# A cheaper exponential on VectorE for 94 tiles, a fused mixer step and zero-weight filler matmuls in a two-layer transformer kernel

## The chip, the cores and the metric

The kernel runs on one core of a Trainium2 chip. The core has a matrix engine (TensorE, PE in the profile; its weight loads are listed as PEld), a vector engine (VectorE, DVE), a scalar engine for activation functions (ScalarE, ACT), a general engine (GpSimd, POOL) and a queue engine (SyncE, SP) that issues the transfers. They run side by side, each working through its own list of instructions in order, and wait for one another by semaphores. The metric is the device time of one execution in microseconds (us).

## The reference

The sequence has 2048 rows of 448 numbers. Two layers with the same weights are applied; each has an attention block A and a mixer block B, and each block gets a layer norm of the stream and is added to it:

```python
def _A_ref(x, wqkv, wo):          # 16 heads of 28
    q, k, v = split(x @ wqkv)
    p = _softmax(einsum("bhqd,bhkd->bhqk", q, k) * 28 ** -0.5)
    return merge(einsum("bhqk,bhkd->bhqd", p, v)) @ wo

def _B_ref(x, w1, w2, w3, w4):
    h = _gelu(_layernorm(x) @ w1)
    hs = concatenate([h quarters shifted by -1, +1, -2, +2 rows]) @ w2
    x1 = x + hs
    h2 = _gelu(_layernorm(x1) @ w3) @ w4     # 448 -> 1792 -> 448
    return x1 + h2

x = A_x
for layer in range(2):
    x = x + _A_ref(_layernorm(x), A_wqkv, A_wo)
    x = x + _B_ref(_layernorm(x), B_w1, B_w2, B_w3, B_w4)
```

The mixer block is thus given a normalised x, and its own sum x1 starts from that. The GELU is the tanh approximation. Inputs and outputs are bf16.

## The kernel before

**Tiling.** The 2048 rows are 16 row tiles of 128. The stream lies in `x_res` (bf16, 128 x 16 x 448) in on-chip memory for the whole run. Heads are handled in 4 groups of 4; the 4 heads of a group use the four 32-row strips of PE at once. Scores are computed transposed (keys on partitions, 512 query columns), so one score tile is 128 keys x 512 queries of one head, and there are 2048 such tiles in the two layers.

**The attention pipeline.** `t_attention` (L1703 ff.) walks over 821 groups of score tiles. Groups have in turn three and two tiles, which fill banks 0 to 2 and 3 and 4 of the accumulator memory. For group n PE computes the scores (L1722), ACT takes the exponential of the whole group in one instruction into `PT` (L1748), and PE multiplies the result with the values (`t_pv`, L1781; the sums of four heads stay in bank 5, `UBK`). The scores of group n+2 are computed into the banks of group n as soon as these have been read, while ACT works on group n+1.

**The exponential on VectorE.** For the groups in `DVE_TILES` (76 of them) ACT does the first two tiles only and VectorE the third, in `t_dexp` (L1631 ff.). The score is a power of two with an offset. Five instructions make the bits of a bf16 number: L1633 turns the score into a fixed-point integer (`t32`, one buffer) and so frees the bank; L1643 takes the low 16 bits, the fraction f, times a constant; L1644 and L1645 make a cubic correction from it, with two half buffers `gt0` and `gt1` of `gt`, which `tanh_gelu` of the mixer uses too; L1648 adds integer and correction and writes 16 bits into `PTD`. The product with the values is deferred by four groups for such a tile. A score matmul into the third bank waits for L1633 of the group two back.

**The mixer.** `t_mixA` takes the row means and variances (L1278, L1279) and normalises (L1958) for w1; `t_r1` makes the reciprocal root R1 of a row. `t_x1` makes x1 for one row tile: L2027 writes (x - mean) x R1 into `x1b` (fp32); PE multiplies the shifted GELU output with w2; L2046 adds it from the accumulator; L2049 to L2053 make the statistics of x1; L2055 adds `x1b` to `x_res`; L2057 normalises for w3. `t_mixB` multiplies with w3, evicts (L2094, DVE; L2091, ACT in the last tiles), ACT takes the GELU of several row tiles at once (`t_gelu`, L2134), PE multiplies with w4, and the result is added to `x_res` (L2117) or, in the last layer, to the output buffer (L2110), which SP stores.

**What sets the order.** All steps are generators that yield instructions. A planner runs twice; then `follow` reorders each engine's list by numbers written out in `ENGINE_ORDER` and moves some choices (`OTHER`) between ACT and DVE. While it lays out PE's list it calls `keep_pe_busy` (L340 ff.), which puts filler matmuls into stretches that the planner's durations show as empty: 128 x 256 of ones into an accumulator bank that is free (L2169), while the planned use of the last 4 us is under 80%. Where no bank is free there is no filler. These durations only set the order; at run time every engine waits for semaphores alone.

Of the kernel before, what the change touches and what calls it, by code (L numbers as in the profile page):

```python
# [49 lines left out]
class Place(str):  # L50


    KINDS = {"b": 8, "sq": 2, "x1b": 2, "xn": 2, "xT": 2, "gw": 2, "gt": 2, "ob": 2, "ti": 1, "pd": 3}
# [163 lines left out]
class Sched:  # L217
# [122 lines left out]
    def keep_pe_busy(self, until):  # L340
# [3 lines left out]
        if self.pe_mode not in (None, "plain"):  # L344
            idle = max(self.strip_free) + self.SW
            if max(self.cur["pe"], idle) + dur + 0.12 >= until:
                return
            self.cur["pe"] = max(self.cur["pe"], idle)
        while self.cur["pe"] + dur + 0.12 < until:
            t = self.cur["pe"]  # L350
# [5 lines left out]
            pick = None  # L356
            for b in banks:
                if key(b) in self.live:
                    continue
                ds = self.P.deps("pe", reads, [key(b)])  # L360
                if all(d.t_end + self.LAT <= t + 0.02 for d in ds.values()):
                    pick = b
                    break
            if pick is None:
                self.cur["pe"] = t + 0.1
                continue
            self.P.add("pe", lambda e, b=pick: fn(e, b), reads, [key(pick)], t_end=t + dur)
            self.recent.append((t, t + dur))
            self.log.append(("pe", t, t + dur, "fill"))
            self.cur["pe"] = t + dur  # L370
            self.pe_mode = "plain"
            self.strip_free = [self.cur["pe"]] * 4
# [203 lines left out]
    def follow(self, order, other, banks):  # L576
# [27 lines left out]
        new.landed = 0.0  # L604
        P = new.P
        made = {}
        head = {e: 0 for e in ENGS}
        while len(made) < len(ops):
# [51 lines left out]
            else:  # L660
                if e == "pe":
# [3 lines left out]
                    new.strip_free, new.begun = pe[3], pe[4]  # L665
                elif e == "act" and kw.get("tab") is not None:
                    new.act_tab = kw["tab"]
# [45 lines left out]
def build_kernel(nc, A_x, A_wqkv, A_wo, B_x, B_w1, B_w2, B_w3, B_w4, out, n_layers=2):  # L713
    S = A_x.shape[1]
    D = 448
# [16 lines left out]
    EXPA = (0.07826797 * 128) ** (1 / 3)  # L732
    EXPB = EXPA * 0.30457565 / 0.07826797
# [1527 lines left out]
```

## Time and profile before

| | |
|---|---|
| time, median of 3 runs | 1041.9 us (1039.48 to 1047.28) |
| the profiled execution: time, span | 1048.76 us, 1047.0 us |
| ACT busy | 1005.5 us, 96% |
| PE busy (matmul) | 974.1 us, 93% |
| DVE busy | 812.6 us, 78% |
| POOL busy | 57.7 us, 6% |
| mean granted PE clock | 0.980 |

Busy time is the time in which an engine executes something; PE's is modelled, since matmuls overlap in its pipeline. The span runs from the first to the last instruction. A row of the groups names the line of the kernel, the engine, the operation, what it writes and reads, how often it ran, the busy time, the mean duration in ns, and the engine's idle time just before with who ended it. A row of the waits names who waited, for whom, how long in total, how often and how long at most. The granted clock is the share of the full clock at which PE ran.

### The profile page before, as it was taken

Reading aid. Unit: us, or ns where it says so; the run is one execution under the profiler, and the core shown is the slowest. Engines: PE = TensorE matmul, PEld = TensorE weight load, DVE = VectorE, ACT = ScalarE, POOL = GpSimd, SP = SyncE. Lnnn points to the kernel's source line nnn. Section 1 sums busy time; section 2 is a strip of 40 time slices with the busy share of each in tenths; the row PEclk is TensorE's granted clock in tenths of the full one; section 3 lists DMA queues with packets and bytes.
Section 4 is the critical chain, followed back from the end, with each engine's and each line's share of the span. In section 5 each row is a group of like instructions: output and inputs, shape, how many; then the busy total and the mean of one; then the engine's idle time right before and its main releaser. Section 6 shows DMA issues by size and latency. Waiting matters only on the chain.

```text
span 1047.0 us, 23598 instructions
## 1 busy us (share of the span) xinstructions
PE 974.1 (93%) x10240; PEld 369.3 (35%) x10260; DVE 812.6 (78%) x1809; ACT 1005.5 (96%) x942; POOL 57.7 (6%) x80
## 2 busy tenths in 40 slices
PE   8998898989998999999999999988898999999998
PEld 4332222323232243332343443323333233443456
DVE  8977667877888778889788777788988846876674
ACT  7999879999999999999999999999999999999984
POOL 2000000000001001010000000000011000010000
PEclk9999769999999999999999999999999999999999
DMA  5246002001011002101111101311010100110000
GB/s 138 62 124 161 11 12 49 2 16 21 1 39 21 1 2 41 36 2 22 22 52 31 27 11 49 105 41 41 21 37 1 21 19 10 26 22 2 14 3 27
DMA packets 70720, 35.19 MB, mean 34 GB/s; under 512 B 56472, under 2 KB 65048, under 8 KB 70616
## 3 DMA queue, kind: packets, MB, share of 16 engines
q1 hardware_dynamic: 70616, 33.68, 13.5%
q8 instruction: 80, 1.31, 0.5%
q14 instruction: 24, 0.20, 0.1%
HBM read 12.70 MB, written 7.08 MB: 19 GB/s over the span
## 4 chain that ended last, share of the span: by engine, by line
ACT 79%; PE 19%; DVE 1%; DMA 1%; issue 0%; SPq 0%; DVEq 0%
ACT PT L1748 72%; PE ps L1128 6%; PE ps L1722 4%; ACT h2T L2134 4%; PE ps L1781 3%; PE ps L1131 3%; PE ps L1391 1%; ACT gt L1918 1%; PE ps L2169 1%; ACT L2134 1%; DMA wk_raw<-in_A_wqkv_dram 1%; ACT L1748 0%; PE ps L1336 0%; DVE hT L1885 0%; ACT vaug L1461 0%
## 5 line engine op out<-in xcount | busy, mean ns | idle before, releaser
L1748 ACT ACTIVATE PT<-ps 128x1024 bf16<-128x1024 f32 (+1 forms) x821 | 903.0, 1235 | 14.8 <-PE ps L1722 11.3
L1781 PE MATMUL ps<-PT,vaug 128*32 128x512 bf16 (+1 forms) x2221 | 287.8, 369 | 4.1 <-ACT PT L1748 2.6
L1722 PE MATMUL ps<-qT,kT 32*128 32x512 bf16 x1536 | 248.8, 393 | 39.7 <-ACT PT L1748 33.3
L1722 PEld LDWEIGHTS ps<-qT,kT 32*128 32x128 bf16 x1536 | 60.4, 91 | 246.6 <-ACT PT L1748 178.1
L1781 PEld LDWEIGHTS ps<-PT,vaug 128*32 128x32 bf16 x2221 | 82.8, 95 | 121.9 <-issue 78.6
L2094 DVE CAST h2T<-ps 128x512 bf16<-128x512 f32 (+2 forms) x126 | 72.3, 582 | 38.3 <-PE ps L1131 19.7
L1128 PE MATMUL ps<-xT,w 112*128 112x512 bf16 (+6 forms) x483 | 99.2, 318 | 1.4 <-DVE h2T L2094 0.7
L1722 PE MATMUL ps<-kT 32*128 32x256 bf16 (+1 forms) x768 | 83.4, 310 | 13.5 <-ACT PT L1748 11.4
L1131 PE MATMUL ps<-xT,w 112*32 112x512 bf16 (+3 forms) x1172 | 90.8, 346 | 0.5 <-DVE h2T L2094 0.4
L2169 PE MATMUL ps<-ones_bf 128*128 128x256 bf16 x402 | 75.0, 293 | 4.9 <-DVE ones_bf L1158 2.7
L1633 DVE TENSOR_SCALAR t<-ps 128x512 int32<-128x512 f32 x76 | 52.2, 687 | 28.4 <-PE ps L1722 27.6
L1131 PE MATMUL ps<-w,h2T 128*32 128x448 bf16 x948 | 60.3, 353 | 2.0 <-ACT h2T L2134 1.6
L1648 DVE SCALAR_TENSOR_TENSOR PTD<-t,gt 128x512 uint16<-128x512 int32 x76 | 52.2, 687 | 3.0 <-PE ps L1781 1.3
L1128 PEld LDWEIGHTS ps<-xT,w 112*128 112x128 bf16 (+1 forms) x483 | 39.3, 104 | 41.3 <-issue 21.6
L1645 DVE SCALAR_TENSOR_TENSOR gt<-gt 128x512 f16<-128x512 f16 x76 | 52.0, 685 | 1.5
L1644 DVE SCALAR_TENSOR_TENSOR gt<-gt 128x512 f16<-128x512 f16 x76 | 51.9, 683 | 1.3
L1128 PE MATMUL ps<-w,h2T 128*128 128x448 bf16 x211 | 52.1, 355 | 0.0
L1722 PEld LDWEIGHTS ps<-kT 32*128 32x128 bf16 x768 | 23.1, 91 | 78.5 <-ACT PT L1748 60.5
L1391 PE MATMUL ps<-xT,wq_raw 112*32 112x512 bf16 (+1 forms) x576 | 49.2, 366 | 0.6 <-DVE gt L1643 0.3
L2169 PEld LDWEIGHTS ps<-ones_bf 128*128 128x128 bf16 x402 | 33.6, 102 | 43.8 <-issue 19.7
L2134 ACT ACTIVATE h2T<-h2T 128x7168 bf16<-128x7168 bf16 (+2 forms) x9 | 44.9, 5012 | 0.1
L1391 PE MATMUL ps<-xT,wk_raw 112*32 112x512 bf16 (+3 forms) x640 | 43.8, 339 | 0.2 <-DVE hT L1885 0.2
(145 smaller groups left out, 1092.8 us busy)
## 6 DMA issues: line engine op xcount, KB each, us to landing
uin<-uscr SPq DMA_DIRECT2D x20, 256.0 KB, 2.6
uscr<-u_sb SPq DMA_DIRECT2D x12, 256.0 KB, 2.0
uscr<-uin SPq DMA_DIRECT2D x8, 256.0 KB, 2.3
out_dram<-uin SPq DMA_DIRECT2D x16, 112.0 KB, 1.7
w<-in_B_w_dram SPq DMA_DIRECT2D x4, 392.0 KB, 5.4
x_res<-in_A_x_dram SPq DMA_DIRECT2D x3, 448.0 KB, 8.3
w<-in_B_w_dram SPq DMA_DIRECT2D x2, 448.0 KB, 4.7
w<-in_B_w_dram SPq DMA_DIRECT2D x4, 196.0 KB, 6.6
```

The source lines that it names most:

```text
L1128: return e.matmul(out=dst(0, m), lhsT=lhs(0, m), rhs=rhs() if callable(rhs) else rhs, start=start, stop=stop)
L1131: return [e.matmul(out=dst(a, min(m, a + 32)), lhsT=lhs(a, min(m, a + 32)), rhs=rhs() if callable(rhs) else rhs, start=start, stop=stop, t ...
L1391: yield op("pe", c_mm(nw) + Sched.COLT, lambda e, b=b, fc=fc, rows=rows: [e.matmul(out=ps[32 * j:32 * j + 32, bi(b), 0:nw], lhsT=w[0:rows, ...
L1633: yield op("dve", 0.06 + c_ps(512), lambda e: e.tensor_scalar(out=t32[:, :], in0=ps[:, bk, :], scalar1=0.0, scalar2=65536.0, op0=ALU.max, ...
L1645: yield op("dve", c_ps(512), lambda e: e.scalar_tensor_tensor(out=half(x), in0=half(f), scalar=EXPB, in1=half(x), op0=ALU.add, op1=ALU.mul ...
L1648: yield op("dve", 0.06 + c_ps(512), lambda e: e.scalar_tensor_tensor(out=PTD[:, to.n, :].bitcast(mybir.dt.uint16), in0=t32[:, :], scalar=2 ...
L1722: yield op("pe", 0.005 if ph == h else 0.012 + W / 2400.0, lambda e, bk=bk, r0=32 * j, g=g, kc=kc, qt=qt, q0=q0, W=W, c0=W * h: e.matmul(o ...
L1748: yield op("act", e_dur(n), lambda e, b0=b0, p0=p0, cnt=cnt: e.activation(out=PT[:, p0:p0 + cnt, :], in_=ps[:, b0:b0 + cnt, :], func=ACT.E ...
L1781: return e.matmul(out=ps[32 * j:32 * j + 32, UBK, 0:128 * nt], lhsT=vaug[:, vs, 32 * (4 * g + j):32 * (4 * g + j) + 32], rhs=rhs(), start= ...
L2094: yield op("dve", c_ps(NW), lambda e, fch=fch, b=b: e.tensor_copy(out=h2T[:, fch, hoff:hoff + NW], in_=ps[:, bi(b), 0:NW]), reads=[("ps", ...
L2134: yield op("act", c_act(14 * NW), lambda e, c0=c0, NW=NW: e.activation(out=h2T[:, :, c0:c0 + NW], in_=h2T[:, :, c0:c0 + NW], func=ACT.Gelu ...
L2169: SC.fill = (0.13, lambda e, b: e.matmul(out=ps[:, bi(b), 0:256], lhsT=ones_bf[:, :], rhs=ones_bf[:, :].unsqueeze(1).to_broadcast([128, 2, ...
```

## The change

It has five parts.

1. **The exponential on VectorE** has another form of the cubic: a linear step, its square (a product of the buffer with itself), and a step that adds a constant and multiplies with the fraction. It needs one half buffer instead of two, so two tiles can be under way; `t32` gets a second buffer as well. The number of instructions stays five.
2. **94 tiles** instead of 76 go to VectorE.
3. **The mixer's first branch.** x x R1 + hs is made in one step straight from the accumulator, without subtracting the mean. x1 then carries a constant per row (mean x R1), which the later layer norms remove by themselves. The stream keeps this constant; `t_r1` collects it in `OFF`, and the last step subtracts it. `x1b` becomes bf16.
4. **Zero-weight filler.** Where no accumulator bank is free, `keep_pe_busy` adds, to the sums in bank 5 that are open (begun and not ended), a matmul of 32 columns of zero weights per strip.
5. **The order** of all engines is written anew.

```diff
-    KINDS = {..., "gt": 2, "ob": 2, "ti": 1, "pd": 3}
+    KINDS = {..., "gt": 2, "ob": 2, "ti": 2, "pd": 3}
...
             for b in banks:
                 if key(b) in self.live:
                     continue
                 ds = self.P.deps("pe", reads, [key(b)])
                 if all(d.t_end + self.LAT <= t + 0.02 for d in ds.values()):
-                    pick = b
+                    self.P.add("pe", lambda e, b=b: fn(e, b), reads, [key(b)], t_end=t + dur)
+                    self.pe_mode = "plain"
                     break
-            if pick is None:
-                self.cur["pe"] = t + 0.1
-                continue
+            else:
+                opened = [j for j in range(4) if 0 < self.sums[j] < self.summands]
+                if not opened or t + self.SW + dur + 0.12 >= until:
+                    t += 0.1
+                    continue
+                for j in opened:
+                    self.P.add("pe", lambda e, j=j: self.still(e, j), self.still_reads, [(self.sum_key, (j, "still"))], t_end=t + dur)
+                self.pe_mode = "col4"
...
-            ti = yield ("acq", ["ti0"])
+            ti = yield ("acq", ["ti0", "ti1"])
...
-            f = yield ("acq", ["gt0"])
-            x = yield ("acq", ["gt1"])
-            ... tensor_scalar(out=half(f), in0=lo, scalar1=EXPA * 2.0 ** -16, scalar2=None, op0=ALU.mult)
-            ... scalar_tensor_tensor(out=half(x), in0=half(f), scalar=-EXPA, in1=half(f), op0=ALU.add, op1=ALU.mult)
-            ... scalar_tensor_tensor(out=half(x), in0=half(f), scalar=EXPB, in1=half(x), op0=ALU.add, op1=ALU.mult)
+            x = yield ("acq", ["gt0", "gt1"])
+            ... tensor_scalar(out=half(), in0=frac(), scalar1=EXPS * 2.0 ** -24, scalar2=EXPH * 2.0 ** -8, op0=ALU.mult, op1=ALU.add)
+            ... tensor_tensor(out=half(), in0=half(), in1=half(), op=ALU.mult)
+            ... scalar_tensor_tensor(out=half(), in0=half(), scalar=EXPV * 2.0 ** -16, in1=frac(), op0=ALU.add, op1=ALU.mult)
...
-        x1b = sb("x1b", [128, NX1, D], FP32)
+        x1b = sb("x1b", [128, NX1, D], BF16)
...
+            yield op("dve", 0.1, ... tensor_tensor(out=mst[:, sl, MR if L else OFF], in0=mv[:, sl, 0], in1=mst[:, sl, R1], op=ALU.mult)
+            if L:
+                yield op("dve", 0.1, ... tensor_tensor(out=mst[:, sl, OFF], in0=mst[:, sl, OFF], in1=mst[:, sl, MR], op=ALU.add)
...
-            yield op("dve", ... tensor_scalar(out=x1b[:, s.n, :], in0=x_res[:, t, :], scalar1=mv[:, t, 0:1], scalar2=mst[:, t, R1:R1 + 1], op0=ALU.subtract, op1=ALU.mult)
...
-            yield op("dve", ... tensor_tensor(out=x1b[:, s.n, :], in0=x1b[:, s.n, :], in1=ps[:, bi(hb), 0:D], op=ALU.add)
+            yield op("dve", ... scalar_tensor_tensor(out=x1b[:, s.n, :], in0=x_res[:, t, :], scalar=mst[:, t, R1:R1 + 1], in1=ps[:, bi(hb), 0:D], op0=ALU.mult, op1=ALU.add)
...
-                    yield op("dve", ... tensor_tensor(out=obf(o), in0=x_res[:, t, :], in1=ps[:, bi(b), 0:D], op=ALU.add)
+                    yield op("dve", ... scalar_tensor_tensor(out=obf(o), in0=x_res[:, t, :], scalar=mst[:, t, OFF:OFF + 1], in1=ps[:, bi(b), 0:D], op0=ALU.subtract, op1=ALU.add)
...
+            SC.still = lambda e, j: e.matmul(out=ps[32 * j:32 * j + 32, UBK, 0:256], lhsT=zeros[:, :], rhs=ones_bf[:, :].unsqueeze(1).to_broadcast([128, 2, 128]),
+                                             start=False, stop=False, tile_position=(0, 32 * j))
```

In the list of instructions that results, 18 of ACT's exponentials shrink from 1536 to 1024 columns; PE's plain fillers are 389 instead of 402, and 275 zero-weight matmuls of 256 columns come in.

More of the change, by code (lines that the diff above doesn't have):

```diff
@@ L1635, in t_dexp @@
             yield ("sig", ("d1", n))
-            f = yield ("acq", ["gt0"])
-            x = yield ("acq", ["gt1"])
-            def half(r):
-                return gt[:, 256 * r.n:256 * r.n + 256].bitcast(FP16)
-            lo = t32[:, :].bitcast(mybir.dt.uint16).rearrange("p (n two) -> p n two", two=2)[:, :, 0]
-            yield op("dve", c_f2b(512), lambda e: e.tensor_scalar(out=half(f), in0=lo, scalar1=EXPA * 2.0 ** -16, scalar2=None, op0=ALU.mult), reads=[("ti", ti)], writes=[("gt", f), ("gt", x)])
@@ L1644, in t_dexp, with frac @@
-            yield op("dve", c_ps(512), lambda e: e.scalar_tensor_tensor(out=half(x), in0=half(f), scalar=-EXPA, in1=half(f), op0=ALU.add, op1=ALU.mult), reads=[("gt", f)], writes=[("gt", x)])
-            yield op("dve", c_ps(512), lambda e: e.scalar_tensor_tensor(out=half(x), in0=half(f), scalar=EXPB, in1=half(x), op0=ALU.add, op1=ALU.mult),
-                     reads=[("gt", f), ("gt", x)], writes=[("gt", x)])
+            x = yield ("acq", ["gt0", "gt1"])
+            def frac():
+                return t32[:, ti.n, :].bitcast(mybir.dt.uint16).rearrange("p (n two) -> p n two", two=2)[:, :, 0]
@@ L1647, in t_dexp @@
             to = ptd_of[n] = yield ("acq", ["pd0", "pd1", "pd2"])
-            yield op("dve", 0.06 + c_ps(512), lambda e: e.scalar_tensor_tensor(out=PTD[:, to.n, :].bitcast(mybir.dt.uint16), in0=t32[:, :], scalar=2.0 ** -9, in1=half(x), op0=ALU.mult, op1=ALU.add),
+            yield op("dve", 0.06 + c_ps(512), lambda e: e.scalar_tensor_tensor(out=PTD[:, to.n, :].bitcast(mybir.dt.uint16), in0=t32[:, ti.n, :], scalar=2.0 ** -9, in1=half(), op0=ALU.mult, op1=ALU.add),
                      reads=[("ti", ti), ("gt", x)], writes=[pt_key(n, 2)])
-            for r in (f, x, ti):
+            for r in (x, ti):
@@ L1925, in tanh_gelu, with t_r1 @@
                 yield ("rel", r)
-        def t_r1(tiles):
+        def t_r1(L, tiles):
             n = len(tiles)
@@ L1935, in t_r1 @@
                 yield ("sig", ("r1", t))
+            ck = [("off", t) for t in tiles]
+            yield op("dve", 0.1, lambda e: e.tensor_tensor(out=mst[:, sl, MR if L else OFF], in0=mv[:, sl, 0], in1=mst[:, sl, R1], op=ALU.mult),
+                     reads=[("mv", t) for t in tiles] + [("mst1", t) for t in tiles], writes=[("mr", t) for t in tiles] if L else ck)
+            if L:
+                yield op("dve", 0.1, lambda e: e.tensor_tensor(out=mst[:, sl, OFF], in0=mst[:, sl, OFF], in1=mst[:, sl, MR], op=ALU.add),
+                         reads=[("mr", t) for t in tiles] + ck, writes=ck)
         def t_mixA(L, tiles, direct):
@@ L2045, in t_x1 @@
             yield ("sig", ("x1", L, t))
-            yield op("dve", c_ps(D), lambda e, s=s, hb=hb: e.tensor_tensor(out=x1b[:, s.n, :], in0=x1b[:, s.n, :], in1=ps[:, bi(hb), 0:D], op=ALU.add),
-                     reads=[("ps", bi(hb)), ("x1b", s)], writes=[("x1b", s)], touch=[hb])
+            yield op("dve", 0.06 + c_ps(D), lambda e, t=t, s=s, hb=hb: e.scalar_tensor_tensor(out=x1b[:, s.n, :], in0=x_res[:, t, :], scalar=mst[:, t, R1:R1 + 1], in1=ps[:, bi(hb), 0:D], op0=ALU.mult, op1=ALU.add),
+                     reads=[("ps", bi(hb)), ("x", t), ("mst1", t)], writes=[("x1b", s)], touch=[hb])
             yield ("rel", hb)
@@ L2109, in w4_tile @@
                     o = yield ("acq", ["ob0", "ob1"])
-                    yield op("dve", c_ps(D), lambda e, t=t, b=b, o=o: e.tensor_tensor(out=obf(o), in0=x_res[:, t, :], in1=ps[:, bi(b), 0:D], op=ALU.add),
-                             reads=[("ps", bi(b)), ("x", t)], writes=[(("uin",), o)], touch=[b])
+                    yield op("dve", c_ps(D), lambda e, t=t, b=b, o=o: e.scalar_tensor_tensor(out=obf(o), in0=x_res[:, t, :], scalar=mst[:, t, OFF:OFF + 1], in1=ps[:, bi(b), 0:D], op0=ALU.subtract, op1=ALU.add),
+                             reads=[("ps", bi(b)), ("x", t), ("off", t)], writes=[(("uin",), o)], touch=[b])
                     yield ("rel", b)
```

72 lines of the change are left out of this document (44 added, 28 removed), and 506 rows, old and new, of tables (DVE_TILES, ENGINE_ORDER).

## The prediction

> **What bounds the kernel now.** I read the page first: busy times, the row of the granted clock and the chain that ended last.
>
> ```profile
> span 1047.0 us, 23598 instructions
> PE 974.1 (93%) x10240; PEld 369.3 (35%) x10260; DVE 812.6 (78%) x1809; ACT 1005.5 (96%) x942; POOL 57.7 (6%) x80
> PEclk9999769999999999999999999999999999999999
> ACT 79%; PE 19%; DVE 1%; DMA 1%; issue 0%; SPq 0%; DVEq 0%
> ```
>
> ACT is busy for 1005.5 of 1047.0 us and holds 79% of the chain, so what comes off ACT comes off the time, and a wait of ACT goes onto it. The clock row has one dent, in slices 5 and 6. Next, who makes ACT wait, and what its exponentials cost by shape:
>
> ```profile
> ACT PT L1748 <- PE ps L1722: 11.3, 20, 1.6
> ```
>
> ```profile
> L1748 ACT ACTIVATE PT<-ps 128x1536 bf16<-128x1536 f32 x333 | 495.8, 1489 | 5.6 <-PE ps L1722 4.4 <-PE ps L1781 0.6
> L1748 ACT ACTIVATE PT<-ps 128x1024 bf16<-128x1024 f32 x485 | 494.9, 1064 | 9.0 <-PE ps L1722 6.9 <-PE ps L1781 1.8
> ```
>
> The largest wait, 11.3 us in 20 pieces, is for the score matmuls, and the exponentials are 990.7 us of ACT's work. A group of three tiles of 512 columns costs ACT 1489 ns, and 1064 ns when VectorE takes the third tile.
>
> ACT's 41.5 us of idle time lie in few places. Two of them are the first 50 us and the end, a stage without exponentials (columns: stretch, its length, busy us of PE, PEld, DVE, ACT and POOL, then the clock, DMA share and GB/s):
>
> ```profile
> 0.00:50.00 50.00, 45.95 (x604) 21.01 (x607) 43.25 (x148) 42.71 (x47) 10.06 (x22) 1.00 0.40 99
> ...
> 1016.00:1047.00 31.00, 28.17 (x270) 19.38 (x262) 14.65 (x36) 11.86 (x40) 4.50 (x7) 1.00 0.07 23
> ```
>
> The start leaves ACT idle for 50.00-42.71 = 7.3 us (loads and first projections). In the end's 31.00 us PE is busy for 28.17 and ACT for 11.86, so 19.1 us of ACT's idle time belong to PE. The dent in the clock holds most of the rest. I cut the trace at the points where the clock changed:
>
> ```profile
> 99.29:102.70 3.41, 1.89 (x13) 0.60 (x14) 3.34 (x6) 3.41 (x4) 0.00 (x0) 1.00 0.34 98
> 102.70:109.53 6.83, 6.83 (x40) 1.66 (x38) 4.63 (x10) 5.41 (x5) 0.00 (x0) 0.50 0.30 66
> 116.36:119.77 3.41, 2.12 (x21) 0.62 (x21) 3.34 (x7) 3.41 (x5) 0.00 (x0) 1.00 0.00 0
> 119.77:123.18 3.41, 3.37 (x26) 0.86 (x26) 0.91 (x3) 2.24 (x2) 0.00 (x0) 0.50 0.00 0
> 123.18:126.60 3.42, 2.14 (x26) 0.60 (x21) 3.35 (x6) 3.35 (x4) 0.00 (x0) 1.00 0.24 77
> 126.60:150.49 23.89, 23.42 (x113) 5.32 (x111) 13.78 (x24) 17.46 (x16) 0.00 (x0) 0.50 0.04 12
> 208.52:211.93 3.41, 1.88 (x22) 0.63 (x21) 3.38 (x7) 3.41 (x5) 0.00 (x0) 1.00 0.00 0
> 211.93:215.34 3.41, 3.41 (x23) 0.89 (x14) 2.58 (x7) 2.81 (x4) 0.93 (x1) 0.50 0.00 0
> 966.27:969.69 3.42, 2.34 (x16) 1.16 (x15) 2.33 (x7) 3.41 (x2) 0.48 (x1) 1.00 0.02 5
> 969.69:973.10 3.41, 3.41 (x51) 2.03 (x50) 0.76 (x3) 3.39 (x2) 0.00 (x0) 0.50 0.00 0
> ...
> 754.64:758.05 3.41, 2.42 (x30) 0.86 (x34) 3.25 (x7) 3.41 (x4) 0.00 (x0) 1.00 0.00 0
> 758.05:761.46 3.41, 3.17 (x32) 1.01 (x21) 3.07 (x8) 3.41 (x4) 0.96 (x1) 1.00 0.02 4
> ```
>
> Each of the five stretches at half clock follows a piece of 3.41 us in which PE was busy for 1.88 to 2.34 us (55% to 68%); after a piece with 2.42 us (71%) the clock stayed whole. At half clock PE is full and ACT waits: 6.83-5.41, 3.41-2.24, 23.89-17.46, 3.41-2.81 and 3.41-3.39 make 1.42+1.17+6.43+0.60+0.02 = **9.6 us** of ACT idle. The execution took 1048.76 us, 1.8 us more than its span and 6.9 us more than the median 1041.9 of the runs shown (1039.48 to 1047.28). I see nothing else in the trace that could differ so much between runs, so my estimate is that the median run lost 9.6-6.9 = 2.7 us to the clock.
>
> **The change, part by part.**
>
> *18 more tiles on VectorE (76 to 94).* The order of the changed kernel has 315 exponentials of 1536 columns and 503 of 1024, against 333 and 485: 18 x (1489-1064) ns = **-7.65 us** of ACT. What else ACT does changes by single instructions (two evictions into xT and one row normalisation go to VectorE, one square and one weight copy come), most of them ahead of the first exponential. Each is between 0.5 and 0.8 us; I take 0, ends -1 and +1.
>
> *The new polynomial and mixer, on VectorE.* Rows for the old and the nearest new operations:
>
> ```profile
> L1648 DVE SCALAR_TENSOR_TENSOR PTD<-t,gt 128x512 uint16<-128x512 int32 x76 | 52.2, 687 | 3.0 <-PE ps L1781 1.3
> L1633 DVE TENSOR_SCALAR t<-ps 128x512 int32<-128x512 f32 x76 | 52.2, 687 | 28.4 <-PE ps L1722 27.6
> ...
> L1645 DVE SCALAR_TENSOR_TENSOR gt<-gt 128x512 f16<-128x512 f16 x76 | 52.0, 685 | 1.5
> L1644 DVE SCALAR_TENSOR_TENSOR gt<-gt 128x512 f16<-128x512 f16 x76 | 51.9, 683 | 1.3
> ...
> L1643 DVE TENSOR_SCALAR gt<-t 128x512 f16<-128x512 uint16 x76 | 31.9, 420 | 1.3
> ...
> L2055 DVE TENSOR_TENSOR x_res<-x_res,x1b 128x448 bf16<-128x448 bf16 x32 | 19.5, 613 | 0.0
> L2046 DVE TENSOR_TENSOR x1b<-x1b,ps 128x448 f32<-128x448 f32 x32 | 19.5, 614 | 5.0 <-PE ps L1131 2.2 <-PE ps L1128 2.2
> ...
> L1922 DVE SCALAR_TENSOR_TENSOR hT<-gt,hT 112x512 bf16<-112x512 f32 x28 | 19.0, 680 | 4.6 <-ACT gt L1918 4.6
> ...
> L1441 DVE SCALAR_TENSOR_TENSOR qT<-ps,sc,qT 128x512 bf16<-128x512 f32 x24 | 17.8, 742 | 5.5 <-PE ps L1131 2.7 <-PE ps L1781 2.0 <-PE ps L1128 0.5
> ...
> L2057 DVE TENSOR_SCALAR xn<-x1b,mv,mst 128x448 bf16<-128x448 f32 x32 | 15.9, 501 | 5.7 <-POOL mst L2053 5.6
> L2027 DVE TENSOR_SCALAR x1b<-x_res,mv,mst 128x448 f32<-128x448 bf16 x32 | 15.8, 503 | 1.1 <-POOL mst L1932 0.9
> ...
> L1958 DVE TENSOR_SCALAR xn<-x_res,mv,mst 128x448 bf16<-128x448 bf16 x32 | 11.0, 390 | 4.1 <-POOL mst L1955 3.8
> L1406 DVE TENSOR_TENSOR sq<-kT 128x512 bf16<-128x512 bf16 x26 | 10.6, 415 | 0.5 <-ACT kT L1403 0.4
> ...
> L2051 DVE TENSOR_SCALAR mst<-mv 128x1 f32<-128x1 f32 x32 | 4.7, 148 | 0.7
> ```
>
> A tile cost 687+420+683+685+687 = 3162 ns. Now the first three-operand step becomes a product of two 16-bit tensors, priced by L1406 at 415; the other takes the fraction straight from the integer tile (every second 16-bit word), for which I keep 685 (L1643 reads the same words at 420, L1648 has an integer operand at 687, so nothing nearby is dearer): 2894 ns, 268 less. 76 x 268 = -20.4 us; 18 x 2894 = +52.1 us.
>
> Per mixer tile L2027 goes (-503). L2046 becomes a three-operand step with a scalar from memory: L1441 has one and takes 742 against L1922's 680, so +62. L2055 has only bf16 operands now, a 448/512 part of L1406's work: between 363 and 415, I take 385 (-228). L2057 becomes like L1958 (-111). That is -780 x 32 = -25.0 us. The 16 output steps (L2110) get the same scalar, +1.0; 16 small row operations at about 148 ns, +2.4. **VectorE: -20.4+52.1-25.0+1.0+2.4 = +10 us**, on an engine that idles for 234 us. It hides under ACT, so I book 0. That cover is thinnest in the first layer's attention, which has no mixer work to save:
>
> ```profile
> 101.00:151.00 50.00, 45.88 (x288) 11.62 (x289) 31.62 (x55) 40.35 (x37) 0.00 (x0) 0.66 0.10 27
> 151.00:210.00 59.00, 53.03 (x457) 17.26 (x455) 47.61 (x97) 58.85 (x58) 3.04 (x3) 1.00 0.10 23
> 210.00:363.00 153.00, 140.69 (x1237) 45.80 (x1238) 124.39 (x239) 152.40 (x145) 6.53 (x8) 0.99 0.08 17
> ```
>
> VectorE has 203.6 us in these 262 (78%). Six of the new tiles lie there (17.4 us), and 33 old ones give back 8.8: 212 of at most 262, or 81%. It stays below full. What a late VectorE costs is shown by those that waited for the tile's integers:
>
> ```profile
>   PEld ps L1722: 4.8, 15
> ```
>
> 15 waits of 0.32 us in 76 tiles. In proportion, 94 tiles make 5.9 us; these waits are PE's, and ACT's own waits name PE only, so I take 0 with ends 0 and +6. The second integer buffer lets a tile's first step, which frees the score bank, run before the preceding tile is finished, and the half buffer no longer blocks the GELU; both speak for 0.
>
> *The zero-weight filler.* PE gets 389 plain fillers instead of 402 and 275 new strip matmuls, in groups of up to four, some 69 groups.
>
> ```profile
> L2169 PE MATMUL ps<-ones_bf 128*128 128x256 bf16 x402 | 75.0, 293 | 4.9 <-DVE ones_bf L1158 2.7 <-DVE h2T L2094 0.8 <-DVE xT L1342 0.5
> ```
>
> A group should hold PE busy about as long as one filler of the same 256 columns, 293 ns, so PE gets (69-13) x 0.293 = +16 us of busy time out of 73 us idle. To lift the five pieces ahead of the half clock from 1.88..2.34 to 2.42 us takes 0.54+0.30+0.28+0.54+0.08 = 1.7 us, six groups in the right places; the order puts some 23 groups between the 50th and the 180th exponential, where four of the five lie. They are issued just when no bank is free for a plain filler. I take two thirds of the clock loss as gone: **-6.4 us** in the profiled execution, -1.8 in the median run. Ends: 0, and the whole 9.6. A filler ahead of a score matmul delays it by at most its 0.3 us, and the scores have the whole next exponential, over 1 us, to be ready.
>
> [...]
>
> *The new order.* The tail after the last score matmul holds the same matmuls but for one output-projection block whole instead of in strips, so 31 us stay. The weight loads are issued in another order on SP, but all long before their use. I book 0, ends -3 and +3, less than the 41.5-7.3-19.1-9.6 = 5.5 us that ACT idles outside of the start, the end and the half clock.
>
> **Sum.** 1048.76 - 7.65 - 6.4 = 1034.7 for the profiled execution; from the median, 1041.9 - 7.65 - 1.8 = 1032.5. I forecast **1033 us**.
>
> **The rivals.**
> *The clock stays whole and the order is tighter*: 1048.76-7.65-9.6-3 = **1028**. For it: 1.7 us of fillers suffice. Against: the piece at 754.64 us, at 71%, stood just above the five, and where the pieces begin need not be the same in each run.
> *The fillers prevent nothing* (zero weights don't count, or come where no hole is): 7.65 us from ACT and as many of the half-clock stretches as before or some more: 1041.9-7.65 = 1034 up to 1048.76-7.65 = 1041; I give it **1039**. For it: the earlier fillers were there and the clock fell all the same.
> *VectorE is late, slower than before*: tiles stand closer now (492 to 498, 694 to 698 every second group). One place decides: the tile's first step holds the third score bank, so if it runs behind the preceding tile's four other steps, the scores for the group after next wait and then ACT. At 0.32 us each, 24 late tiles use up the 7.65 us; with 70 of 94 late it is 1032.5+0.32 x 70 = **1055**. Against: 15 of 76 now, and +10 us on 234 idle.
>
> **How the numbers follow.** Chances: forecast 0.42 (its own range 1029 to 1038), whole clock 0.22, fillers in vain 0.26, late VectorE 0.10. The range 1024 to 1045 leaves out the last and the ends of the others, under 0.2. About 1% (10.4 us) is what a measurement here can tell from no change: faster than 1031.5 are most of the second case and a third of the first, 0.36; slower than 1052.3 is the last, 0.09; the rest is 0.55.
>
> **What would show it.** ACT busy near 998 us with 315 and 503 exponentials; the product at about 415 ns, the fused step near 676, the residual add near 385, VectorE near 823; no or one stretch at half clock between 100 and 150 us, and ACT's wait for L1722's successor well under 11 us. Wrong would be: stretches at half clock after pieces with fillers in them; waits of PE for the tile's integers far above 6 us; or ACT idle in the first layer's attention at full clock.

## The result: 1030.9 us, and the profile after

The changed kernel takes **1030.87 us** (median of 6 executions, 1027.68 to 1031.54), against 1044.15 us for the kernel before in executions beside it: ratio 0.9862, 95% interval 0.9827 to 0.9897. The forecast was 1033 us, from 1024 to 1045. The profiled execution took 1029.99 us, with a span of 1028.2 us.

The page of the changed kernel: span, busy times, granted clock, and the chain that ended last by engine and (its first entries) by line.

```profile
span 1028.2 us, 24176 instructions
PE 976.8 (95%) x10502; PEld 376.4 (37%) x10516; DVE 817.5 (80%) x1884; ACT 995.1 (97%) x941; POOL 52.4 (5%) x81
PEclk9999999999999999999999999999999999999999
ACT 88%; PE 10%; DMA 1%; DVE 1%; issue 0%; SPq 0%; DVEq 0%
```

ACT holds 88% of the chain instead of 79%, PE 10% instead of 19%: the dent in the clock row is gone, and with it half of the chain's time on PE. Where the 18.8 us of span went is seen best when the trace is cut at the first and after the last exponential (stretch, length, then busy us of PE, PEld, DVE, ACT and POOL, the clock, DMA share and GB/s). First before, then after:

```profile
0.00:21.77 21.77, 18.44 (x255) 11.62 (x256) 16.90 (x74) 14.73 (x21) 7.78 (x20) 1.00 0.56 142
21.77:1011.32 989.55, 923.47 (x9659) 335.87 (x9677) 777.69 (x1691) 974.47 (x880) 45.41 (x53) 0.98 0.13 32
1011.32:1047.00 35.68, 32.16 (x329) 21.77 (x327) 18.04 (x45) 16.33 (x43) 4.50 (x7) 1.00 0.06 20
```

```profile
0.00:23.55 23.55, 21.33 (x266) 12.97 (x267) 16.58 (x77) 14.89 (x23) 6.96 (x19) 0.93 0.54 131
23.55:992.54 968.99, 923.72 (x9915) 341.74 (x9928) 784.34 (x1761) 964.86 (x880) 41.70 (x55) 1.00 0.14 33
992.54:1028.20 35.66, 31.77 (x322) 21.73 (x321) 16.59 (x46) 15.32 (x41) 3.72 (x7) 1.00 0.05 17
```

The start is 1.8 us longer, the tail is the same, and the middle is 20.6 us shorter. In the middle ACT works 974.47-964.86 = 9.6 us less, and idles 968.99-964.86 = 4.1 us instead of 989.55-974.47 = 15.1 us, that is 11.0 us less. So between these two profiles about half of the gain is work taken from ACT, and half is idle time of ACT, of which 9.6 us lay in half-clock stretches before. The profiled execution of the kernel before was one of its longer ones, with a clock of 0.980 where 68 executions have 0.988 in the mean; the medians lie closer together than these two profiles.

The groups of the changed kernel that answer to the terms of the prediction (busy us, mean ns):

```profile
L1772 ACT ACTIVATE PT<-ps 128x1024 bf16<-128x1024 f32 x503 | 509.5, 1066 | 2.3 <-PE ps L1746 2.3
L1772 ACT ACTIVATE PT<-ps 128x1536 bf16<-128x1536 f32 x315 | 469.8, 1491 | 1.5 <-PE ps L1746 1.0
...
L1655 DVE TENSOR_SCALAR t<-ps 128x512 int32<-128x512 f32 x94 | 64.6, 687 | 27.0 <-PE ps L1746 26.3
L1669 DVE SCALAR_TENSOR_TENSOR gt<-gt,t 128x512 f16<-128x512 f16 x94 | 64.3, 687 | 1.5
L1672 DVE SCALAR_TENSOR_TENSOR PTD<-t,gt 128x512 uint16<-128x512 int32 x94 | 64.2, 685 | 2.3 <-PE ps L1805 0.9
...
L1666 DVE TENSOR_SCALAR gt<-t 128x512 f16<-128x512 uint16 x94 | 39.2, 419 | 1.6
L1668 DVE TENSOR_TENSOR gt<-gt 128x512 f16<-128x512 f16 x94 | 39.0, 418 | 1.6
...
L2073 DVE SCALAR_TENSOR_TENSOR x1b<-x_res,mst,ps 128x448 bf16<-128x448 bf16 x32 | 21.4, 673 | 8.4 <-PE ps L1147 6.0 <-PE ps L1150 2.1
...
L2198 PE MATMUL ps<-ones_bf,zeros 128*32 128x256 bf16 x275 | 18.8, 279 | 0.3 <-DVE gt L1669 0.3
...
L2084 DVE TENSOR_SCALAR xn<-x1b,mv,mst 128x448 bf16<-128x448 bf16 x32 | 12.4, 391 | 5.4 <-POOL mst L2080 4.9
L2082 DVE TENSOR_TENSOR x_res<-x_res,x1b 128x448 bf16<-128x448 bf16 x32 | 11.9, 376 | 0.0
```

A VectorE tile now costs 687+419+418+687+685 = 2896 ns. The waits of ACT for scores in the changed kernel (us in total, times, longest):

```profile
ACT PT L1772 <- PE ps L1746: 3.3, 9, 0.5
```

They were 11.3 us in 20 pieces. And who waited for the integers that VectorE makes (us, times), 4.8 us in 15 pieces before:

```profile
  PEld ps L1746: 7.2, 21
```

### The profile page after: what moved, and what is told of

Same layout as the page of the kernel before. It is cut to its first block, busy times and chain, and to the rows that moved or that the text cites. A ratio compares the mean times of both kernels' runs of the same rounds, so it can differ in the third digit from the quotient of the medians.

```text
span 1028.2 us, 24176 instructions
## 1 busy us (share of the span) xinstructions
PE 976.8 (95%) x10502; PEld 376.4 (37%) x10516; DVE 817.5 (80%) x1884; ACT 995.1 (97%) x941; POOL 52.4 (5%) x81
## 4 chain that ended last, share of the span: by engine, by line
ACT 88%; PE 10%; DMA 1%; DVE 1%; issue 0%; SPq 0%; DVEq 0%
ACT PT L1772 80%; ACT h2T L2161 4%; PE ps L1147 4%; PE ps L1150 2%; PE ps L1746 2%; ACT gt L1942 1%; PE ps L1413 1%; PE ps L1805 1%; ACT L2161 1%; ACT L1772 1%; DMA xT<-xn 1%; DMA x_res<-in_A_x_dram 0%; PE ps L1358 0%; ACT vaug L1483 0%; DVE st L1300 0%
## 5 line engine op out<-in xcount | busy, mean ns | idle before, releaser
L1772 ACT ACTIVATE PT<-ps 128x1024 bf16<-128x1024 f32 (+1 forms) x821 | 893.5, 1227 | 3.9 <-PE ps L1746 3.3
L1746 PE MATMUL ps<-qT,kT 32*128 32x512 bf16 x1536 | 244.6, 384 | 28.2 <-ACT PT L1772 20.6
L1147 PE MATMUL ps<-xT,w 112*128 112x256 bf16 (+6 forms) x493 | 100.7, 319 | 0.3
L1150 PE MATMUL ps<-xT,w 112*32 112x512 bf16 (+3 forms) x1132 | 87.6, 343 | 0.8 <-DMA xT<-xn 0.6
L1655 DVE TENSOR_SCALAR t<-ps 128x512 int32<-128x512 f32 x94 | 64.6, 687 | 27.0 <-PE ps L1746 26.3
L2196 PE MATMUL ps<-ones_bf 128*128 128x256 bf16 x389 | 71.3, 284 | 1.4 <-DVE ones_bf L1177 1.2
L1672 DVE SCALAR_TENSOR_TENSOR PTD<-t,gt 128x512 uint16<-128x512 int32 x94 | 64.2, 685 | 2.3 <-PE ps L1805 0.9
L1669 DVE SCALAR_TENSOR_TENSOR gt<-gt,t 128x512 f16<-128x512 f16 x94 | 64.3, 687 | 1.5
L1147 PEld LDWEIGHTS ps<-xT,w 112*128 112x128 bf16 (+1 forms) x493 | 40.7, 104 | 40.7 <-issue 22.1
L1147 PE MATMUL ps<-w,h2T 128*128 128x448 bf16 x209 | 51.6, 355 | 0.0
L1413 PE MATMUL ps<-xT,wq_raw 112*32 112x512 bf16 (+1 forms) x576 | 45.0, 361 | 0.3 <-issue 0.3
L1150 PEld LDWEIGHTS ps<-xT,w 112*32 112x32 bf16 (+1 forms) x1132 | 35.6, 95 | 15.5 <-DVE h2T L2121 2.4
```

The lines of the kernel that those rows point to most:

```text
L1147: return e.matmul(out=dst(0, m), lhsT=lhs(0, m), rhs=rhs() if callable(rhs) else rhs, start=start, stop=stop)
L1150: return [e.matmul(out=dst(a, min(m, a + 32)), lhsT=lhs(a, min(m, a + 32)), rhs=rhs() if callable(rhs) else rhs, start=start, stop=stop, t ...
L1413: yield op("pe", c_mm(nw) + Sched.COLT, lambda e, b=b, fc=fc, rows=rows: [e.matmul(out=ps[32 * j:32 * j + 32, bi(b), 0:nw], lhsT=w[0:rows, ...
L1655: yield op("dve", 0.06 + c_ps(512), lambda e: e.tensor_scalar(out=t32[:, ti.n, :], in0=ps[:, bk, :], scalar1=0.0, scalar2=65536.0, op0=ALU ...
L1669: yield op("dve", c_ps(512), lambda e: e.scalar_tensor_tensor(out=half(), in0=half(), scalar=EXPV * 2.0 ** -16, in1=frac(), op0=ALU.add, o ...
L1672: yield op("dve", 0.06 + c_ps(512), lambda e: e.scalar_tensor_tensor(out=PTD[:, to.n, :].bitcast(mybir.dt.uint16), in0=t32[:, ti.n, :], sc ...
```

## The experiments

All kernels ran in rounds with the kernel before on the same chip; the ratio is to that. Each execution has a mean granted clock beside its time. Over 170 executions of eleven kernels a line with one slope for all, time = T + 0.718 us per 0.001 of missing clock, leaves 0.7 us of scatter; T is then a kernel's time at full clock, an estimate by that line. This splits each kernel's mean time into work and clock:

| kernel | median us | ratio, 95% | T at full clock, us | mean loss to the clock, us |
|---|---|---|---|---|
| before (68 executions) | 1041.4 | | 1034.3 | 8.4 |
| after (12 executions, two batches) | 1030.5 | 0.986 and 0.990 | 1028.1 | 3.1 |
| after, no zero-weight filler | 1032.99 | 0.9897 [0.985, 0.9944] | 1028.0 | 4.7 |
| before, with zero-weight filler | 1037.36 | 0.9949 [0.9919, 0.9979] | 1035.6 | 2.7 |
| before, filler, 18 exponentials cut | 1034.63 | 0.9926 [0.9899, 0.9952] | 1031.0 | 3.7 |
| after, third tiles on ACT again | 1050.96 | 1.009 [1.0058, 1.0121] | 1049.3 | 2.8 |
| after, ACT time put back on own banks | 1037.46 | 0.9962 [0.993, 0.9994] | 1035.9 | 2.6 |
| after, dearer VectorE | 1033.61 | 0.993 [0.9897, 0.9962] | 1031.4 | 3.5 |
| after, all three put back | 1046.71 | 1.0032 [0.9997, 1.0068] | 1038.0 | 9.7 |
| after, 16-column sums | 1030.20 | 0.9896 [0.9865, 0.9928] | 1028.1 | 1.9 |
| after, 64-column sums | 1027.87 | 0.9854 [0.9811, 0.9898] | 1027.9 | 0.2 |

From before to after the time at full clock fell by 6.2 us and the loss to the clock by 5.3 us.

**The zero-weight filler: taken out of the changed kernel.** With an empty list of open sums, `keep_pe_busy` lays out 398 plain fillers and no zero-weight ones.

```diff
-                opened = [j for j in range(4) if 0 < self.sums[j] < self.summands]
+                opened = []
```

> The changed kernel without the zero-weight matmuls (398 plain fillers instead of 389, everything else in the same order on every engine). Theory, the zero-weight filler keeps the clock whole: half-clock stretches come back, mean clock 0.98 to 0.99, and the time goes from 1031 to between 1034 and 1041 us. Rival, the new order and the shorter exponentials fill PE enough by themselves: clock at least 0.995 and 1029 to 1033 us.

Measured: 1032.99 us, 2.1 us above the 1030.87 of the changed kernel, with overlapping intervals. The time is the rival's; the mean clock of the six executions, 0.9935, is a little below the rival's 0.995. The stretch from 100 to 150 us, first of this run, then of the changed kernel:

```profile
100.00:150.00 50.00, 43.14 (x339) 13.01 (x340) 39.48 (x75) 48.49 (x46) 0.00 (x0) 0.93 0.13 27
138.50:141.90 3.40, 2.58 (x18) 0.87 (x17) 2.93 (x5) 3.40 (x4) 0.00 (x0) 1.00 0.01 2
141.90:148.70 6.80, 6.80 (x38) 1.60 (x38) 4.54 (x9) 5.29 (x6) 0.00 (x0) 0.50 0.01 2
```

```profile
100.00:150.00 50.00, 44.77 (x417) 14.42 (x412) 41.03 (x78) 50.00 (x48) 0.00 (x0) 1.00 0.16 30
```

Without it one stretch of 6.8 us at half clock comes back, in which ACT idles for 6.80-5.29 = 1.5 us. That is far from the 6.83+3.41+23.89 = 34.1 us of half clock that the profiled execution of the kernel before had there, and the mean loss is 4.7 us where the kernel before loses 8.4. So in the new kernel most of the clock is kept without the zero-weight filler. By the medians the filler is worth about 2 us, which the intervals do not tell from nothing.

**The zero-weight filler alone, in the kernel before.** The edits to `keep_pe_busy`, the zero weights and the counting of open sums are those of the change; nothing else is.

```diff
+                opened = [j for j in range(4) if 0 < self.sums[j] < self.summands]
+                for j in opened:
+                    self.P.add("pe", lambda e, j=j: self.still(e, j), ...)
```

> The kernel before with only the zero-weight filler added (396 plain fillers and 290 zero-weight matmuls, in its own order). Theory, the filler alone removes the half clock: mean clock above 0.99 and 1035 to 1041 us against 1044 of the kernel before on this chip. Rival, zero weights don't count or come in the wrong places: clock 0.98 to 0.985 and no change within 2 us.

Measured: 1037.36 us. In the old order the filler cuts the mean loss to the clock from 8.4 to 2.7 us, and costs 1.3 us at full clock. So here matmuls with zero weights kept the clock up. The two runs together say that the filler and the rest of the change save the same loss: either one takes out a good part of it, and what the second adds is small.

**ACT's 18 tiles, first attempt.** ACT does the third tile of the 18 groups again, beside VectorE.

```diff
+                full = 3 if n in AGAIN else cnt
-    in_=ps[:, b0:b0 + cnt, :], ...
+    in_=ps[:, b0:b0 + full, :], ...
```

> The changed kernel, but in the 18 new groups ACT takes the exponential of all three tiles again; the third result is never read, since VectorE still makes that tile. So ACT's work is that of before, and all else stays. Theory, the 18 shorter exponentials are worth their difference: 18 x 0.425 = +7.7 us, 1037 to 1040 us. Rival, the gain came from the clock and ACT had time to spare: 1031 to 1033 us.

Measured: 1050.96 us, some 20 us instead of 7.7. The waits of ACT in this run:

```profile
ACT PT L1779 <- DVE t L1661: 10.7, 15, 1.3
ACT PT L1779 <- PE ps L1752: 9.7, 20, 1.3
```

The first row is new. The kernel's bookkeeping lets an engine read an accumulator bank only when a reader on another engine is done with it, so 15 of the 18 exponentials waited for VectorE's first step on the third bank, and the score matmuls after them came late too. The run priced its own wait, not ACT's time, so it says nothing about the 7.7 us.

**ACT's 18 tiles, without the third bank.** Ahead of each of the 18 exponentials ACT takes 452 elements of the group's own first bank once more, into a place that nobody reads. Order and fillers stay those of the changed kernel.

```diff
+ [e.activation(out=PT[:, p0 + 2, 0:k], in_=ps[:, b0, 0:k], func=ACT.Exp, ...) for k in ks] +
  [e.activation(out=PT[:, p0:p0 + cnt, :], in_=ps[:, b0:b0 + cnt, :], func=ACT.Exp, ...)]
```

> The changed kernel, with one more ScalarE exponential ahead of each of the 18 exponentials that the change shortened: 128x452 elements of the group's own first bank, into a place that nobody reads. By the start-to-start times in the trace of after (1331 ns for 1536 elements, 904 ns for 1024) it takes the 427 ns that the third tile took, but holds no bank that VectorE or TensorE waits for, and the order and the fillers stay those of after. Theory (ScalarE sets the pace, 427 ns a tile): 18 x 0.427 = 7.7 us, 1038.5 us, ratio to before 0.992 to 0.997. Rival 1 (the 20 us of the run that took the third tile twice are what ScalarE time costs here, through the clock and late groups): 1045 to 1051 us. Rival 2 (TensorE sets the pace): 1031 us.

Measured: 1037.46 us, at full clock 1035.9-1028.1 = 7.8 us above the changed kernel. The middle, from the first to the last exponential:

```profile
23.15:999.85 976.70, 925.12 (x9915) 342.29 (x9928) 784.94 (x1761) 972.62 (x898) 41.70 (x55) 1.00 0.14 32
```

ACT is busy 972.62-964.86 = 7.8 us longer, idle as before (4.1 us), and the stretch is 7.7 us longer. In this kernel time added to ACT passes one to one into the total.

**The 18 shorter exponentials in the old order.** The kernel before with the filler, and the 18 exponentials cut to two tiles. The third tiles are left out: no engine computes them.

```diff
+ cnt = min(cnt, 2) if n in SHORT else cnt
```

> The kernel before with the zero-weight filler alone (1037.4 us in the batch before), and the 18 exponentials cut to two tiles, in the old order and with the old VectorE chain of 3162 ns for the other 76. The third tiles of the 18 groups are left out: nobody computes them. Theory (the gain is ScalarE time plus clock, the new order and the cheaper VectorE are worth nothing): 1037.4 - 18 x 0.427 = 1029.7 us, within 2 us of after. Rival 1 (without the new order the shorter exponentials turn into waits for scores): 1034 to 1037 us.

Measured: 1034.63 us, 2.7 us below the filler alone, 4.6 us at full clock. Neither 1029.7 nor clearly the rival: the middle of both, filler alone first:

```profile
21.66:1005.60 983.94, 929.42 (x9943) 340.92 (x9961) 778.24 (x1691) 973.74 (x880) 45.41 (x53) 0.99 0.14 32
```

```profile
21.30:995.32 974.02, 921.97 (x9943) 340.00 (x9961) 777.86 (x1691) 966.89 (x880) 45.41 (x53) 1.00 0.14 32
```

ACT works 6.9 us less, about as it should, but still idles for 974.02-966.89 = 7.1 us, 3.0 us more than in the changed kernel, and waits for scores 16 times (5.1 us) instead of 9 times (3.3 us). In the old order part of the time saved is spent waiting. In the changed kernel the scores come in time; that the new order alone does it, and not the second buffers too, is likely but was not run. The medians differ by less than these two profiles (9.9 us), since the profile with the filler alone had a clock of 0.99 and the other 1.00.

**Dearer VectorE.** The square and the residual add become three-operand instructions.

```diff
- tensor_tensor(out=half(), in0=half(), in1=half(), op=ALU.mult)
+ scalar_tensor_tensor(out=half(), in0=half(), scalar=0.0, in1=half(), op0=ALU.add, op1=ALU.mult)
- tensor_tensor(out=x_res[:, t, :], in0=x_res[:, t, :], in1=x1b[:, s.n, :], op=ALU.add)
+ scalar_tensor_tensor(out=x_res[:, t, :], in0=x_res[:, t, :], scalar=0.0, in1=x1b[:, s.n, :], op0=ALU.add, op1=ALU.add)
```

> The changed kernel with the square written as a three-operand step (about 685 instead of 418 ns, 94 times) and the residual add of the mixer likewise (about 613 instead of 376 ns, 32 times): +25.1 and +7.6, together +32.7 us of VectorE, to 850 us. Theory, VectorE is hidden: 1030 to 1034 us. Rival, with 94 tiles VectorE stands close to the path and its cheaper steps were needed: 1038 us or more, with longer waits of PE for the tile's integers (7.2 us now) and ACT idle at full clock.

Measured: 1033.61 us, 2.7 us above the changed kernel. The rows that show the edit:

```profile
L1668 DVE SCALAR_TENSOR_TENSOR gt<-gt 128x512 f16<-128x512 f16 x94 | 64.0, 685 | 1.6
...
L2082 DVE SCALAR_TENSOR_TENSOR x_res<-x_res,x1b 128x448 bf16<-128x448 bf16 x32 | 19.4, 609 | 0.0
```

That is 25.0 + 7.5 = 32.5 us more on VectorE, of which 3.3 us reach the total at full clock: a tenth. At that rate the 10 us that the change was reckoned to add would be worth about 1 us, an estimate.

**All three put back.** No zero-weight filler, the 452-element exponentials, and the dearer VectorE instructions, in the changed kernel. Its order, its fused mixer, the second buffers and the 18 more tiles on VectorE are left.

> The changed kernel without the zero-weight filler, with the 452-element exponential ahead of the 18 shortened ones, and with the square and the residual add as dearer VectorE instructions (33 us of VectorE time more). What is left of the change is the new order and the fused mixer. Theory (that remainder is worth nothing): 1030.9 + 2 (filler) + 7.7 (ScalarE) + 2.5 (VectorE) = 1043 us, ratio to before 0.998 to 1.002. Rival (the new order is worth some 5 us by itself, by fewer waits and evictions moved): 1037 to 1039 us.

Measured: 1046.71 us, ratio 1.0032 with 1 in its interval, and 3.7 us above the 1043 of the theory, which had put the filler at 2 us only. At full clock it is 1038.0; less the 3.3 us of the dearer VectorE, 1034.7, against 1034.3 before. What is left of the change gains nothing in sum; the order alone was not run. The loss to the clock is back too, 9.7 us against 8.4 (7.9 against 7.8 without the three longest executions, 1066.45, 1053.66 and 1053.61 us).

**The half clock at the start.** The profiled execution of the changed kernel has one half-clock piece, in front of the first exponential, which that of the kernel before had not. Of the seven profiles in the new order with the sums as they are, six have it. The pieces in question, and what PE did in the first of them:

```profile
9.00:12.40 3.40, 3.14 (x50) 2.78 (x49) 3.07 (x11) 2.69 (x5) 0.42 (x1) 1.00 1.13 243
12.40:15.80 3.40, 3.40 (x33) 1.30 (x37) 3.25 (x16) 0.91 (x2) 1.40 (x2) 0.50 0.47 160
```

```profile
L1358 PE MATMUL ps<-ident,xn 128*112 128x128 bf16 x16 | 2.1, 235 | 0.0
L1237 PE MATMUL ps<-ones_bf,h2T 112*112 112x1 bf16 x15 | 1.4, 183 | 0.0
L1237 PE MATMUL ps<-ones_bf,w 112*112 112x1 bf16 x16 | 1.1, 189 | 0.0
L2196 PE MATMUL ps<-ones_bf 128*128 128x256 bf16 x1 | 0.3, 269 | 0.0
```

PE counts as busy for 3.14 of 3.40 us (92%), yet half clock follows. But 31 of the matmuls have a single column: all groups together stream 16 x 128 + 31 + 256 = 2335 columns, and L1237 takes 183 ns for one column where a filler takes 284 for 256. So the theory: the clock goes by columns streamed, not by the time in which PE has an instruction. For full speed, an estimate from two rows of this kernel: a matmul L1147 (112*128) takes 383 ns with 512 columns and 274 with 256, that is 0.43 ns a column, so 2335 columns are 1.0 of 3.40 us, a share of 0.29. The edit makes the 32 sums of L1237 64 columns wide, of which the first is read:

```diff
-    out=ps[0:112, bi(b), ng * i + k:ng * i + k + 1], ..., rhs=ones_bf[0:112, 0:1]
+    out=ps[0:112, bi(b), WC * (ng * i + k):WC * (ng * i + k + 1)], ..., rhs=ones_bf[0:112, 0:WC]
```

> The changed kernel, with the 32 one-column matmuls of the weight sums (L1237) made 64 columns wide, the first of which is read. They take hardly longer each, but stream 2048 columns in place of 32 at 9 to 12 us, where the only half-clock piece of after begins. If the clock goes by columns streamed in a piece of 3.41 us (0.29 of full speed there in after, to about 0.5 here): no half clock at 12 to 16 us, the first exponential up to 1.7 us earlier, 1029.2 us. Rival (the clock goes by how long TensorE is busy, 92% in that piece, or by chance): the half-clock piece stays, 1030 to 1032 us.

Measured: **1027.87 us**, the fastest kernel of this study. The same pieces:

```profile
9.00:12.40 3.40, 3.15 (x60) 2.73 (x61) 2.72 (x7) 2.10 (x5) 0.00 (x0) 1.00 1.12 260
12.40:15.80 3.40, 3.40 (x68) 1.61 (x64) 3.30 (x18) 2.63 (x4) 1.40 (x2) 1.00 0.36 121
21.22:990.13 968.91, 923.72 (x9915) 341.70 (x9928) 784.28 (x1761) 964.90 (x880) 41.70 (x55) 1.00 0.15 33
```

```profile
L1239 PE MATMUL ps<-ones_bf,h2T 112*112 112x64 bf16 x15 | 1.6, 208 | 0.0
L1239 PE MATMUL ps<-ones_bf,w 112*112 112x64 bf16 x16 | 1.1, 214 | 0.0
```

The wide sums take 208 and 214 ns instead of 183 and 189. PE is as busy as in the changed kernel (3.15 us), the clock stays whole, and the first exponential starts at 21.22 instead of 23.55 us; the middle is unchanged (968.91 us). The pieces need not begin at the same point: the half-clock piece at the start began at 12.4 us in the first profile of the changed kernel and at 12.0 us in its second, below. So one profile proves little. To see whether the width or merely the shifted work did it, the sums were made 16 columns wide, and the changed kernel was run again beside that.

```diff
-            WC = 64
+            WC = 16
```

> The changed kernel with the 32 one-column matmuls of the weight sums made 16 columns wide in place of 64, addressed and read as in the 64-column run: 512 columns in place of 2048. If the columns streamed in a piece of 3.41 us decide the clock: 512 columns are 0.06 of full speed in that piece, it stays near 0.35, and the half-clock piece stays, 1031 us as the changed kernel. Rival (the other addressing, or the mere shift of the work, took the half-clock piece away in the 64-column run): no half clock, 1028 us.

> The changed kernel once more, on the chip and in the rounds of the 16-column run, to compare with. Both theories: 1031 us, one half-clock piece at 10 to 16 us in most runs, clock 0.996 to 0.998.

Measured: 1030.20 us with 16 columns, 1030.21 us for the changed kernel beside it. A mean clock of 1.000 was granted in 1 of 12 executions with one column (the two batches), in 2 of 6 with 16, and in 5 of 6 with 64 (the sixth had 0.998). So with the wide sums the clock was kept. That it is their width, and not the addressing that the 16-column run shares with them, is made likely by the 4 of 6 executions with 16 columns that lost clock; six executions against six do not settle it.

The second run of the changed kernel showed one thing more. Its profiled execution took 1039.18 us, and a stretch near 170 us is most of the difference. This run first, with its half-clock piece at the start, then the first profile of the same kernel:

```profile
12.00:15.40 3.40, 3.40 (x40) 1.36 (x36) 2.57 (x15) 2.03 (x3) 1.40 (x2) 0.50 0.44 149
...
165.60:169.00 3.40, 3.27 (x15) 0.97 (x15) 2.35 (x5) 3.40 (x4) 0.00 (x0) 1.00 0.55 102
169.00:196.30 27.30, 27.30 (x139) 6.64 (x141) 13.68 (x28) 18.29 (x18) 0.00 (x0) 0.50 0.00 1
```

```profile
165.60:169.00 3.40, 3.29 (x18) 1.03 (x17) 2.02 (x3) 3.40 (x4) 0.00 (x0) 1.00 0.85 159
169.00:196.30 27.30, 26.09 (x224) 8.90 (x222) 21.13 (x44) 27.30 (x28) 0.00 (x0) 1.00 0.00 1
```

PE was 96% and 97% busy in the piece ahead, and in one of the two 27.3 us at half clock followed, in which ACT idled for 27.30-18.29 = 9.0 us. The order of the instructions is the same, but the same times do not hold the same work. The half-clock stretches that begin and end inside these two profiles and that of the kernel before last 3.41, 6.83, 23.89 and 27.3 us, each a whole number of pieces of 3.41 us. Counted from them, a piece begins at 165.61 us in the first execution and at 165.97 in the second, while one group of score matmuls begins at 164.95 and at 165.93. The work thus lies 0.6 us differently in the piece. In the first attempt at ACT's 18 tiles it lies as in the first execution, within 0.1 us, and there too 27.3 us at half clock follow, from 169.3 us. None of the other six profiles in the new order has the work within 0.2 us of that place, and none has half clock there.

## Why the prediction was right, step by step

- **The number, 1033 against 1030.9: near, in part by luck.** At full clock the kernel gained 6.2 us where 7.65 were forecast, and the loss to the clock fell by 5.3 us where 1.8 were forecast for the median run. The second term was a third of its true size, and the smaller gain at full clock hid part of that.
- **ACT, 18 x (1489-1064) ns = -7.65 us: right.** Putting that time back costs 7.8 us at full clock. What the prediction did not see is the condition: in the kernel before with the filler the same 18 cuts bring 4.6 us.
- **What else ACT does, 0: right, but a second effect of the same size was left out.** ACT's work in the middle fell by 9.6 us, 2.0 more than the tiles. An exponential that follows without a wait overlaps the end of the one before: 1331 ns from start to start against a duration of 1491, so 0.16 us of overlap. ACT waited for scores 9 times instead of 20; 11 waits fewer give 11 x 0.16 = 1.8 us of overlap, an estimate that accounts for the 2.0. By this estimate a wait of ACT costs its length and 0.16 us.
- **VectorE +10 us, booked 0: right.** It came to 817.5 us, 5 more than before, where about 823 was forecast; why the total rose by half only is not shown. The single prices hold: product 418 ns (415 forecast), tile 2896 (2894), fused step 673 (676), residual add 376 (385), row normalisation 391 (390). Waits of PE for a tile's integers rose to 7.2 us in 21 pieces, where the proportion gave 5.9. All of it cost about 1 us, by the estimate from the dearer VectorE. The rival "VectorE is late", 1055 us, falls: even 32.5 us more on VectorE cost 3.3 us.
- **The zero-weight filler, -6.4 us in the profiled execution and -1.8 in the median run: the mechanism right, the second figure wrong.** The step that failed is the estimate that the median run lost only 2.7 us to the clock. It took the 9.6 us of ACT idle in the half-clock stretches for all that the profiled execution lost. By the line through 68 executions of the kernel before, its profiled execution (clock 0.980) lost 1048.76-1034.3 = 14.5 us, and its median 7.1. What makes up the 4.9 us between 9.6 and 14.5 is shown in part only: in the middle ACT idles 11.0 us more than after the change, and 11 more waits cost an estimated 1.8 us of overlap. With 7.1 for 2.7 and the same two thirds, the sum from the median would have been 1041.9-7.65-4.7 = 1029.5 in place of 1032.5.
- **Who saved the clock: half wrong.** The prediction gave the saving to the filler. The filler alone does it (8.4 to 2.7 us), but so, in good part, does the rest of the change without it (4.7 us). With all three put back the loss is 9.7. The rival "the fillers prevent nothing", 1039 us, falls by the run with the filler alone.
- **The sign of a half clock, PE 55% to 68% busy: wrong as a threshold.** Half clock followed pieces with 2.58 of 3.40 us (76%) and with 3.14 of 3.40 us (92%).
- **The new order, 0 with ends -3 and +3: right as far as shown.** 1034.7 against 1034.3 us with the three put back, which is the order together with the mixer, the buffers and the 18 tiles. The tail stayed, 35.66 against 35.68 us. The order, or the buffers with it, is needed all the same for some 3 of the 7.7 us.
- **Not foreseen**: the half-clock piece at the start; the first exponential starts 1.8 us later in the profiled execution. The forecast of 1033 us left a third of the clock loss standing, the case of 1028 us none. The result lies between them, and the execution with a clock of 1.000 took 1027.68. That this case's sum gives the same number is luck: it counted 9.6 us of clock and 3 of order, where the line gives 14.5 and the runs no gain by the order.

## What to carry to other kernels

Before pricing a change, set the times of many executions against their mean granted clock: here the line takes out nearly the whole scatter, all but 0.7 us, and what is left (1034.3 to 1028.1 us) is the work. Here a cut on the engine that bounds the kernel came through in full (7.8 us) only where the work that feeds it was handed over in time, and in part (4.6 us) where it was not; so such a cut and the order belong together. And an experiment that puts work back must not put a wait back with it: look at the waits of each run before believing its time.

## What the runs showed of the hardware that was not expected

- **The clock is the scatter.** The kernel before ran with mean clocks from 0.974 to 0.998, and its times follow them at 0.7 us per 0.001 (correlation 0.987 over 68 executions). 0.001 of mean clock is 2.1 us at half clock, so a microsecond at half clock costs about a third of a microsecond here; in the five stretches of the kernel before ACT was still busy for 31.3 of 41.0 us.
- **A busy PE was granted half clock.** With one-column matmuls PE was busy for 3.14 of 3.40 us (92%) by the profile, and half clock followed; the same 32 matmuls at 64 columns took about as long (208 against 183 ns) and the clock was 1.000 in 5 of 6 executions instead of 1 of 12. The half-clock piece did not begin at a fixed time from the kernel's start: at 12.4 us in one execution of the changed kernel and at 12.0 us in another.
- **Matmuls with zero weights kept the clock up**: the filler alone brought the kernel before from 8.4 to 2.7 us of loss.
- **The pieces before half clock share a low count of weighted columns.** In all twelve profiles, each matmul's columns in a piece of 3.41 us were multiplied by its rows and columns of the array (the 32*128 of a row) over 128*128. The 20 full-clock pieces that half clock followed come to 1566 to 2824 such columns; of the other 3544 pieces 48 have as few, and half have more than 4500. Without the weight the 20 have 2244 to 11522 columns, and PE is busy for 55% to 96% of them, so neither busy time nor columns alone sets them apart. The lowest piece between 162 and 170 us has 2225 and 2201 in the two executions with 27.3 us at half clock, and 2265 to 3269 in the other seven profiles in the new order.
- **Open**: the weighted count was found in these traces afterwards, no run tests it, and 48 pieces with a count as low kept the clock. What decides the clock is not shown.
